# Moving the first stage boundary of a hand-scheduled loop in front of one projection, with two loads and a store behind it

## The chip, the cores and the metric

The kernel runs on one core of one Trainium2 chip. The metric is the device time of one execution in microseconds (us); the number used is the median of several runs. The core has five instruction streams that run beside each other: TensorE (PE, with its weight loads shown as PEld), VectorE (DVE), ScalarE (ACT), GpSimd (POOL) and SyncE (SP). They meet only through semaphores. SP computes nothing here: it issues loads from DRAM and waits for them. ACT and POOL also issue some transfers.

## The reference

An input `x` of 2048 tokens with 640 features goes through two mixers, and a gate per token blends them: `out = g * a + (1 - g) * b`. Mixer `b` is a sliding, dilated attention. Mixer `a`, which takes most of the time, works through 64 segments of 32 tokens, one after the other, with 8 memory rows that each segment hands to the next:

```python
for s in range(n_seg):
    h = concat([mem, x[:, 32*s : 32*s+32, :]])             # 8 + 32 rows of 640
    q, k, v = h @ Wq, h @ Wk, h @ Wv                       # 32 heads of 192 each
    p = softmax(where(mask, q @ k.T * scale, -1e9))
    o = (p @ v) @ Wo
    mem = o[:, :8, :]
    outs.append(o[:, 8:, :])
```

Since `mem` comes out of the whole segment, segment s + 1 can't begin its projections before segment s has ended.

## The kernel before, in words

Mixer `b` runs first and leaves its share of the result in DRAM (`bsc_dram`). A pre-pass then computes, for all segments at once, the projections of the last 8 tokens of each segment (the "z" rows, `zpk_dram`). What is left per segment is a block of 32 rows, which the method `part_a` works through with the function `segment(prev, s, nxt, looped)`: segment 0 straight, then a loop over 62 segments, then the last one straight, then the output projection of the z rows (`part_z`). Only the loop has stages.

Within a segment the 6144 columns of Q, of K and of V come in three thirds of 2048. `m_qk(i, kcs)` is a projection on PE: i = 0, 2, 4 are the thirds of Q and i = 1, 3, 5 the thirds of K. For each of the five 128-row chunks (kc) of the weights it issues a group of four matmuls that run side by side on the array (line 708). `c_qk(i)` is ACT's copy of the result out of PSUM (line 715), `t_qk(i)` the DVE transpose of it into the layout that attention reads (lines 725 and 728). `m_v(t, kcs)` (line 805) and `c_v(t)` (line 813) do the same for V. Attention is done in two halves h of the heads: `scores(h)` (line 759), `e_exp(h)` (lines 767 and 768), `e_sum(h)` (row sums on PE, line 783), `e_norm(h)` (lines 791 to 796), `pv_half(h)` (lines 829 and 835), and `o_group` is the output projection (line 868).

Not all weights fit on the core. 21 pieces, of 192 or 256 KB, are streamed from DRAM in every segment through a ring of seven buffers `wst`. `release(keys)` marks a buffer free after the last matmul that reads it, and at that place in the program `pump()` puts SP's load of the piece that comes seven places later in the list `STREAM` (line 463). So a load belongs to the place in the program where an older piece is used up, and SP issues it once PE has got there. The second K third, `m_qk(3)`, uses up the pieces ("k", 1, 0, 0) and ("k", 1, 3, 1); the two loads that it sets off bring ("v", 1, 1, 0) and ("v", 1, 4, 1), which `m_v(1)` reads in its second and its last chunk.

The order on every engine is the order of the program text (`manual_schedule`); nothing is rearranged. Semaphores are set back in turns: the loop body has four stages, split by three calls of `stage` (each is a `stage_boundary`) and by the loop's own edge. An engine may enter a stage only when all five engines have reported that they are through with everything of the stage two before it, landed transfers included. The line where an engine makes that report is given by `done(engine, ...)` (a `previous_stage_wait`): there it waits for its own work of the stage before the present one and reports. `done(SP)` thus waits for the landing of the loads that SP issued in that stage. In the trace the instructions of the boundaries and of `done` have the line of the loop, 993. Stage 0 runs from the loop's edge to the first boundary (line 912), stage 1 to the second (line 929), stage 2 to the third (line 960), stage 3 to the edge.

Around the change: `load_vz(s)` loads the z rows of V for `pv_half` (issued by POOL, line 644), `store(prev)` stores the mixed output rows of the segment before (issued by ACT, line 672) from the tile `aG`, which `mix` fills on DVE early in the segment.

Of the kernel before, what the change touches and what calls it, by code (L numbers as in the profile page):

```python
# [26 lines left out]
class _K:  # L27
# [558 lines left out]
    def part_a(self):  # L586
        nc, tc, KC, S = self.nc, self.tc, self.KC, self.S
# [3 lines left out]
        with ctx:  # L591
# [51 lines left out]
            def load_vz(s):  # L643
                nc.gpsimd.dma_start(vz[:], row(self.zpk_dram, s)[:, 768:1152])
# [21 lines left out]
            def store(s, last=False):  # L666
                dst = self.out2d[bass.ds(32 * s, 32), :].rearrange("t (j f) -> j t f", j=4)
                if last:
                    for jj in range(4):
                        nc.scalar.dma_start(dst[jj, 0:24], a4[32 * jj:32 * jj + 24, 0:160])  # L670
                else:
                    nc.scalar.dma_start(dst, a4[:, 0:160])
# [5 lines left out]
            def segment(prev, s, nxt, looped=False):  # L678
# [3 lines left out]
                def stage(*engines):  # L682
                    if looped:
                        tc.stage_boundary()
                    done(*engines)

                def done(*engines):
                    if looped:
                        for e in engines:
                            tc.previous_stage_wait(e)  # L690


                def burst(ms):
                    if looped and len(ms) > 1:
                        key = ms[-1].ins.name
                        for m in ms[:-1]:
                            tc.no_tile_sem_insts.add(m.ins.name)
                            tc.add_to_no_dep_group(key, m.ins)
                        tc.declare_fence(ms[-1].ins, group=key)

                def m_qk(i, kcs):
                    p, m = i // 2, "qk"[i % 2]
                    if i not in pqs:
                        pqs[i] = Ms[i % 2] if p == 1 or i == 4 else X[:, i % 2]
                    pq = pqs[i]
                    for kc in kcs:
                        sl = self.qk_columns((m, p, kc))
                        burst([nc.tensor.matmul(pq[32 * j:32 * j + 32, :], lhsT=hT[:, kc, :], rhs=sl[j],  # L708
                                                start=(kc == 0), stop=(kc == KC - 1), tile_position=(0, 32 * j),
                                                skip_group_check=True) for j in range(4)])  # L710
                        self.release(self.parts((m, p, kc)))

                def c_qk(i, part=None):
                    if part is None:
                        nc.scalar.copy(st[i], pqs[i])  # L715
                    elif part == 0:
                        nc.scalar.copy(st5[0], pqs[i][:, 0:256].rearrange("p (b x) -> p b x", b=4))
                    else:
                        nc.scalar.copy(st5[1], pqs[i][:, 256:512])

                def t_qk(i, part=None):

                    p = i // 2
                    if i % 2 == 0:
                        nc.vector.transpose(P[p][:, 1:5, :, :].rearrange("p b c i -> p c b i"), st[i])  # L725
                    else:
                        c0, c1 = (16 * p % 32, 16 * p % 32 + 16) if part is None else (8 * part, 8 * part + 8)
                        nc.vector.transpose(KT[:, c0:c1, :].rearrange("p c k -> p (c k)"),  # L728
                                            st[i] if part is None else st5[part])
# [178 lines left out]
                t_qk(0); t_qk(1)  # L908
                m_qk(2, range(KC)); c_qk(2); t_qk(2)
                done(SP)  # L910
                m_qk(3, range(KC)); c_qk(3); t_qk(3)
                stage(POOL)
                if prev is not None:
                    load_vz(s)
                    store(prev)
                m_qk(4, range(KC))
                done(PE, ACTE, DVE)
                m_qk(5, (0, 1, 2))
# [70 lines left out]
            ctx.enter_context(tc.manual_schedule(engines=set(ALL)))  # L989
            self.start_stream()  # L990
            segment(None, 0, 1)
            self.sent -= len(STREAM)
            with tc.For_i(0, nseg - 2, 1, hint_engines=(), iteration_sync="staggered", head_align_engines=ALL, name="seg") as i:
                ahead = self.sent
                segment(i, i + 1, i + 2, True)
                self.sent -= len(STREAM)
                assert self.sent == ahead
            segment(nseg - 2, nseg - 1, None)

            def last():  # L1000
# [116 lines left out]
```

## Time and profile before

| what | value |
|---|---|
| median of 3 runs | 1722.83 us (1720.89 to 1736.27) |
| the profiled execution | 1735.46 us, span of its core 1733.6 us |
| granted TensorE clock, mean | 0.978 |
| matmuls | 37477 |
| moved over the span | 438.32 MB, 253 GB/s on average |

A line of the profile names the engine, the source line, the operation and the tiles (written <- read). In a list of waits, "A L1 <- B L2: 86.2, 58, 1.5" says that A, before its instruction of L1, waited for B's L2 86.2 us in all, 58 times, 1.5 us at the longest; "issue" as releaser means that the profile shows no instruction on which it waited: the engine's own sequencer had not handed the instruction over. A "q" after an engine is its sequencer. In a timeline the columns are start and duration in us, engine, line, operation, tiles and count, and in brackets the idle time before. The busy time of matmuls is modelled: four side by side, of 0.38 us each, start every 0.22 us.

### The profile page before, as it was taken

How to read it: one execution, taken by the hardware profiler on the slowest of the kernel's cores; microseconds unless marked ns; L12 is line 12 of the kernel's file. 1: busy time of each engine (PE TensorE's matmuls, PEld its weight loads, DVE VectorE, ACT ScalarE, POOL GpSimd, SP SyncE). 2: the span in 40 equal slices, each digit the busy share in tenths (PEclk: the TensorE clock that was granted, in tenths of full speed). 3: DMA queues.
4: the chain of work that ended last, by engine and by line, in shares of the span. 5: the costliest groups of instructions: out<-in, count | busy, mean ns of one | idle time of the engine just before them, and what ended most of it. 6: DMA issues, size and time to landing. Idle time of an engine off the chain costs nothing. (4 is left out here: it accounts for less than half of the span.)

```text
span 1733.6 us, 91514 instructions
## 1 busy us (share of the span) xinstructions
PE 1488.5 (86%) x37477; PEld 846.2 (49%) x37477; DVE 745.1 (43%) x1808; ACT 721.8 (42%) x1737; POOL 143.7 (8%) x275
## 2 busy tenths in 40 slices
PE   6898997985789889888888898888888888888879
PEld 3454553432345455545545555555554455454447
DVE  4556532222344444444444444444444444444420
ACT  3766631211244444444444444444444444444340
POOL 4001000000100000001000000000100000010000
PEclk9999998998899999999999999999999999999989
DMA  6931079598689989899998998999999899988881
GB/s 165 217 89 48 30 184 283 135 259 250 198 284 313 300 294 310 297 292 290 303 298 289 303 306 298 299 296 307 298 301 299 285 300 297 297 289 293 269 221 27
DMA packets 438730, 438.32 MB, mean 253 GB/s; under 512 B 194172, under 2 KB 306820, under 8 KB 438660
## 3 DMA queue, kind: packets, MB, share of 16 engines
q1 hardware_dynamic: 344344, 395.02, 72.1%
q10 hardware_dynamic: 87148, 29.72, 7.0%
q0 software_dynamic: 7168, 12.60, 2.0%
q8 instruction: 51, 0.84, 0.2%
q14 instruction: 19, 0.16, 0.0%
HBM read 402.83 MB, written 39.48 MB: 255 GB/s over the span
## 5 line engine op out<-in xcount | busy, mean ns | idle before, releaser
L708 PEld LDWEIGHTS <-aH 128*32 128x32 bf16 x7680 | 193.4, 97 | 266.1 <-issue 63.0
L805 PE MATMUL psm<-wlate_v,aH 128*32 128x512 bf16 x3200 | 253.6, 381 | 0.0
L868 PEld LDWEIGHTS <-aP 128*32 128x32 bf16 x6144 | 162.4, 96 | 60.0 <-ACT aP L847 18.8
L708 PE MATMUL psx<-wlate_k,aH 128*32 128x512 bf16 x1920 | 191.4, 386 | 0.0
L868 PE MATMUL psm<-wlate_oa,aP 128*32 128x384 bf16 x2560 | 167.0, 327 | 0.0
L708 PE MATMUL psx<-wres_q,aH 128*32 128x512 bf16 x1152 | 95.7, 393 | 78.3 <-issue 30.1
L715 ACT CAST aP<-psx 128x512 bf16<-128x512 f32 x128 | 68.7, 589 | 224.5 <-PE psx L708 224.5
L728 DVE STREAM_TRANSPOSE aK<-aP 128x512 bf16<-128x512 bf16 (+1 forms) x256 | 142.6, 557 | 15.8
L708 PE MATMUL psx<-wst,aH 128*32 128x512 bf16 x768 | 138.8, 385 | 3.0 <-DMA wst<-wscr 3.0
L868 PE MATMUL psm<-wst,aP 128*32 128x384 bf16 (+1 forms) x896 | 128.1, 305 | 6.4 <-DMA wst<-wscr 6.0
L725 DVE STREAM_TRANSPOSE aP<-aP 128x512 bf16<-128x512 bf16 x128 | 91.1, 711 | 95.8 <-ACT aP L715 95.7
L868 PE MATMUL psm<-wlate_ob,aP 128*32 128x256 bf16 x2688 | 125.7, 273 | 0.7 <-issue 0.7
L805 PE MATMUL psm<-wst,aH 128*32 128x512 bf16 x640 | 125.1, 383 | 0.0
L805 PEld LDWEIGHTS <-aH 128*32 128x32 bf16 x3840 | 91.0, 97 | 63.3 <-issue 1.8
L708 PE MATMUL psm<-wlate_q,aH 128*32 128x512 bf16 x1408 | 105.2, 379 | 1.2 <-ACT aP L715 1.0
L847 DVE CAST aP<-psx 128x128 bf16<-128x128 f32 (+2 forms) x192 | 75.5, 421 | 64.2 <-PE psx L835 64.0
L768 DVE TENSOR_TENSOR aK<-aK,aSel 128x224 bf16<-128x224 bf16 x128 | 35.3, 276 | 151.3 <-ACT aK L767 151.3
L847 ACT CAST aP<-psS 128x384 bf16<-128x384 f32 (+2 forms) x192 | 65.3, 374 | 79.6 <-PE psx L835 77.9
L708 PE MATMUL psm<-wst,aH 128*32 128x512 bf16 x512 | 98.1, 379 | 0.0
L783 PE MATMUL psS<-aK,aSel 128*32 128x160 bf16 (+1 forms) x1024 | 36.1, 216 | 70.5 <-DVE aK L728 59.9
L813 ACT CAST aP<-psm 128x512 bf16<-128x512 f32 x128 | 75.4, 589 | 49.1 <-PE psS L759 49.1
L767 ACT ACTIVATE aK<-psS 128x224 bf16<-128x224 f32 x128 | 46.1, 360 | 117.7 <-PE psS L759 117.7
(164 smaller groups left out, 2762.3 us busy)
## 6 DMA issues: line engine op xcount, KB each, us to landing
wst<-wscr SPq DMA_DIRECT2D x965, 256.0 KB, 4.0
wst<-wscr SPq DMA_DIRECT2D x384, 192.0 KB, 3.2
aP<-zpk_dram SPq DMA_DIRECT2D x64, 192.0 KB, 2.9
zpk_dram<-ZS ACTq DMA_DIRECT2D x5, 2048.0 KB
aVz<-zpk_dram POOLq DMA_DIRECT2D x64, 96.0 KB, 4.5
wlate_k<-in_A_Wk_dram SPq DMA_DIRECT2D x8, 512.0 KB
wres_q<-in_A_Wq_dram SPq DMA_DIRECT2D x7, 512.0 KB
wst<-in_A_Wk_dram SPq DMA_DIRECT2D x14, 256.0 KB
```

The costliest lines, as they stand in the source:

```text
L708: burst([nc.tensor.matmul(pq[32 * j:32 * j + 32, :], lhsT=hT[:, kc, :], rhs=sl[j], start=(kc == 0), stop=(kc == KC - 1), tile_position=(0, ...
L715: nc.scalar.copy(st[i], pqs[i])
L725: nc.vector.transpose(P[p][:, 1:5, :, :].rearrange("p b c i -> p c b i"), st[i])
L728: nc.vector.transpose(KT[:, c0:c1, :].rearrange("p c k -> p (c k)"), st[i] if part is None else st5[part])
L767: nc.scalar.activation(E, pSs[h][:, :, 0:112], ACT.Exp, scale=scale_a)
L768: nc.vector.tensor_tensor(out=E, in0=E, in1=self.mask[h].unsqueeze(1).to_broadcast([128, 2, 112]), op=ALU.mult)
L783: ms.append(nc.tensor.matmul(out, lhsT=self.bones[:, j:j + 1].to_broadcast([128, 32]), rhs=rhs, start=(z == 0), stop=(z == 1), tile_positi ...
L805: burst([nc.tensor.matmul(pvs[t][32 * j:32 * j + 32, :], lhsT=hT[:, kc, :], rhs=sl[j], start=(kc == 0), stop=(kc == KC - 1), tile_position ...
L813: (nc.vector.tensor_copy if t == 0 else nc.scalar.copy)(Px[t], pvs[t][:])
L847: (nc.scalar.copy, nc.vector.tensor_copy)[g](x.rearrange("p (j c q) -> p j c q", j=2, q=32), pairs[g][:, :, 0:240].rearrange("p j (c q) -> ...
L868: ms.append(nc.tensor.matmul(pso[part][32 * jj:32 * jj + 32, 0:n], lhsT=oT_slot(R // 2, j, 3 * (R % 2) + t), rhs=self.o_weights(osl, part, ...
```

## The change

In `segment`, the first boundary, `load_vz` and `store` stand in front of the second K third instead of behind it:

```diff
                 m_qk(2, range(KC)); c_qk(2); t_qk(2)
                 done(SP)
-                m_qk(3, range(KC)); c_qk(3); t_qk(3)
                 stage(POOL)
                 if prev is not None:
                     load_vz(s)
                     store(prev)
+                m_qk(3, range(KC)); c_qk(3); t_qk(3)
                 m_qk(4, range(KC))
                 done(PE, ACTE, DVE)
```

So `m_qk(3)`, its copy, its transpose and the two loads that its `release` calls issue go from stage 0 to stage 1. On ACT's queue the store is issued ahead of `c_qk(3)` and not behind it; on POOL's queue nothing else lies between the two places; on SP's queue the boundary now comes ahead of the two loads. The calls `done(PE, ACTE, DVE)`, `done(SP)` and `done(POOL)` keep their places. The straight segments, which have no stages, change only in the order of the store and `c_qk(3)` on ACT.

## The prediction

> **What bounds the kernel now.** I read first the page's engine shares, then stretches of the loop, then the waits inside it, and last one repetition as a timeline, with what SP and PE do on the loop's line.
>
> ```profile
> PE 1488.5 (86%) x37477; PEld 846.2 (49%) x37477; DVE 745.1 (43%) x1808; ACT 721.8 (42%) x1737; POOL 143.7 (8%) x275
> ```
>
> PE leads, and is idle for 14% of the span. The next view sums each engine's busy time over a stretch: 1100 us of the loop, and one repetition (559.2 to 578.1) which I use as the specimen.
>
> ```profile
> 500.00:1600.00 1100.00, 966.66 (x29588) 556.50 (x29581) 506.05 (x1338) 482.10 (x1281) 95.65 (x176) 1.00 0.91 298
> 559.20:578.10 18.90, 16.59 (x508) 9.55 (x508) 8.71 (x23) 8.29 (x22) 1.62 (x3) 1.00 0.94 304
> ```
>
> The clock is full (1.00), the DMA engines are busy 0.91 of the time, PE is idle about 2 us of 18.9. The view of the instructions on the tile aVz gives the repetition:
>
> ```profile
> L644 POOL DMA_DIRECT2D aVz<-zpk_dram x58: 541/543/557, 510.3 to 1585.2; - x58
> ```
>
> 57 periods in 1074.9 us: 18.86 us each, 62 in all. Where PE's idle time lies, by the list of waits over the same 1100 us, and then SP's own list:
>
> ```profile
> POOL aVz L644 <- issue: 378.9, 58, 7.9
> ...
> PEld L783 <- issue: 86.2, 58, 2.2
> ...
> PE psS L783 <- DVE aK L728: 57.5, 57, 1.6
> ```
> ```profile
> SPq L993 <- DMA wst<-wscr: 160.6, 178, 2.2
> ```
>
> The costliest stop of PE's weight loads (the second row), 86.2 / 58 = 1.49 us per repetition, is ahead of `e_sum(0)` (line 783), the first PE work behind the second boundary, and its releaser is the sequencer. SP in turn loses 160.6 us in its `done` calls, on landings. The specimen shows how the two hang together. SP's and PE's instructions of line 993 around the second boundary, and the timeline:
>
> ```profile
> L993 SPq EVENT_SEMAPHORE  x3: 28/28/28, 568.5 to 568.6; - x3
> L993 PEldq EVENT_SEMAPHORE  x2: 51/51/51, 568.7 to 568.9; - x2
> ```
> ```profile
> 567.41 0.60 PE L805 MATMUL psm<-wlate_v,aH 128*32 128x512 bf16 x8
> 567.90 0.96 DVE L728 STREAM_TRANSPOSE aK<-aP 128x256 bf16<-128x256 bf16 x2
> ...
> 568.93 0.15 PEld L783 LDWEIGHTS <-aSel 128*32 128x32 bf16 x8 [1.41 <-issue]
> 568.96 0.28 PE L783 MATMUL psS<-aK,aSel 128*32 128x160 bf16 x8 [0.94 <-DVE aK L728]
> 568.97 0.69 DVE L813 CAST aP<-psm 128x512 bf16<-128x512 f32 x1
> ...
> 569.05 0.40 PE L805 MATMUL psm<-wst,aH 128*32 128x512 bf16 x2
> ...
> 569.72 0.38 PE L805 MATMUL psm<-wst,aH 128*32 128x512 bf16 x2
> ...
> 570.17 0.21 DVE L796 TENSOR_TENSOR aK<-aK,psS 128x64 bf16<-128x64 bf16 x1
> ...
> 571.29 0.10 PEld L829 LDWEIGHTS <-aP 32*128 32x128 bf16 x4 [0.19 <-ACT aP L813]
> ```
>
> SP reports at 568.6, PE passes at 568.7 to 568.9, `e_sum` starts at 568.96. The two matmul groups from 567.41 were through by 567.41 + 2 x 0.22 = 567.85: PE lost 1.11 us. On which landing did SP wait? The loads of `m_qk(3)`, then the four earlier ones of stage 0 (view of the tile wst, with the time from issue to landing):
>
> ```profile
> L463 SPq DMA_DIRECT2D wst<-wscr x2: 319/320/320, 563.2 to 563.9; - x2
> ...
> DMA to landing us min/median/max: 4.2/4.4/4.6
> ```
> ```profile
> L463 SPq DMA_DIRECT2D wst<-wscr x4: 319/320/365, 560.3 to 562.4; - x4
> ...
> DMA to landing us min/median/max: 3.5/3.8/4.0
> ```
>
> 563.9 + 4.6 = 568.5, the start of SP's three instructions to the tenth. The four others had landed by 562.4 + 4.0 = 566.4. So the second boundary opens when the later load of `m_qk(3)` lands, and that load is one of the two that the change takes out of stage 0.
>
> **The change part by part.** *Second boundary.* SP's `done` has then only the four loads to wait for. It reaches them after its last load of `m_qk(5)`:
>
> ```profile
> 566.81 0.32 SPq L463 DMA_DIRECT2D wst<-wscr  x1
> ```
>
> 566.81 + 0.32 = 567.13, plus some 0.15 for its instructions: 567.3, past 566.4, so nothing is left to wait for. From SP's last instruction to the matmul it takes 0.33 us (568.63 to 568.96): `e_sum` could start at 567.6, and PE gets there at 567.85. The whole stop goes; SP and PE are both moved by the stop below, so the margin of 0.25 stays. Scaled from the specimen (stop 1.41) to the mean (1.49), PE gains 1.11 + 0.08 = 1.19 us per repetition.
>
> *First boundary.* It was free, and is so no longer. The timeline and, below it, line 993 on SP and PE:
>
> ```profile
> 562.75 0.38 PE L708 MATMUL psm<-wst,aH 128*32 128x512 bf16 x2
> ...
> 563.11 0.59 ACT L715 CAST aK<-psm 128x512 bf16<-128x512 f32 x1
> ...
> 564.00 0.54 POOL L644 DMA_DIRECT2D aVz<-zpk_dram  x1 [6.53 <-issue]
> 564.05 0.59 ACT L715 CAST aP<-psm 128x512 bf16<-128x512 f32 x1 [0.36 <-PE psm L708]
> ...
> 564.35 0.57 ACTq L672 DMA_DIRECT2D out_dram<-aG  x1
> ...
> 564.94 0.71 DVE L728 STREAM_TRANSPOSE aK<-aP 128x512 bf16<-128x512 bf16 x1
> ...
> 565.56 0.35 PE L759 MATMUL psS<-aP,aK 128*32 128x40 bf16 x14
> ```
> ```profile
> L993 SPq EVENT_SEMAPHORE  x3: 17/28/278, 562.7 to 562.8; - x3
> ```
> ```profile
> L993 PEldq EVENT_SEMAPHORE  x2: 51/51/51, 563.1 to 563.3; - x2
> ```
>
> SP reports at 562.8 + 0.28 = 563.08 and PE's sequencer passes at 563.1 to 563.3, while the array has `m_qk(3)` (from 562.75) to do, handed over before. Behind the boundary, `m_qk(3)` starts 0.33 after SP's report, at 563.41: PE stands still for 0.66 us. Queued behind it are all later matmuls; ACT (`c_qk(3)`), DVE (`t_qk(3)`) and SP's two loads wait for them. Lower bound: without SP's 0.28, 0.38. Upper bound 0.9: POOL, too, is let go by this boundary, and its longest wait, 7.9, is 1.4 above the mean; one repetition in six like that adds 0.24. I take 0.66, since POOL's mean, 378.9 / 58 = 6.53, is the specimen's.
>
> *Store and load.* POOL's load stays where it is, at the opening of the boundary. ACT's store comes earlier: it takes 0.57 us from about 563.11 + 0.30, so to 563.98, and `c_qk(3)` is wanted only at 564.05 + 0.66. Cost nothing; without that cover it would be 0.57. `t_qk(3)` then ends near 566.1, where `scores(0)` starts at 565.56 + 0.66 = 566.2.
>
> *What is late next.* DVE's chain moves 0.66 later while PE comes 0.53 earlier. `c_v(0)` would end at 568.97 + 0.69 + 0.66 = 570.3 and the second multiplication of `e_norm(0)`, 0.7 after the copy in the present (570.17 + 0.21 - 569.66), at most at 571.0. `pv_half(0)` wants it by 571.29 - 0.53 = 570.76, the start of the part that waits for ACT's copy anyway. Since today's 0.7 holds a wait for ACT, the cost lies between 0 and 0.25; I take 0.05.
>
> Sum per repetition: -1.19 + 0.66 + 0.05 = -0.48 us; times 62, -30 us. From the profiled 1735.46 that is 1705.5; the median of the runs lies 12.6 lower, so 1693.
>
> At one place the Trainium skill speaks against this. "DMA: Bandwidth & Descriptors", section on the anatomy of one DMA, fits a transfer by 2.0 us plus bytes over 436 GB/s, measured on the GpSimd path; for 256 KB that is 2.6 us, an estimate from that page. By it the two loads would land at 566.5, and the sum would be the loss alone, the third rival below. The measured 4.2 to 4.6 us, under load, is against it and decides.
>
> **The rivals.** *The V pieces come too late.* The two loads are issued 0.66 later, at 563.9 and 564.54, and by the same 4.2 and 4.6 land at 568.1 and 569.1. `m_v(1)` wants them at 569.05 - 0.53 = 568.5 and 569.72 - 0.53 = 569.2, so the second has 0.1 to spare. The four loads behind them are slower still:
>
> ```profile
> L463 SPq DMA_DIRECT2D wst<-wscr x4: 320/346/373, 564.9 to 566.8; - x4
> ...
> DMA to landing us min/median/max: 4.4/4.8/4.9
> ```
>
> With 0.4 us more the gain falls to about 0.1 x 62 = 6 us: 1717. For it: a DMA share of 0.94 in the specimen. Against: the four loads ahead of them are issued when they are now, so these two find a shorter queue. Chance 0.17. The specifications in the Trainium skill's "DMA: Bandwidth & Descriptors" give a core about 358 GB/s from HBM; an estimate from that leaves the specimen's 304 GB/s a sixth of room.
>
> *Slower: the second boundary is not the last releaser.* The profile itself puts part of the stop on the transposes of `t_qk(5)` (57.5 us, the third row of the waits). If `e_sum` needs them, it starts at 567.90 + 0.96 + 0.66 = 569.52, 0.56 later than now, and the change costs 35 us: 1758. It decides as soon as the transposes end behind the boundary. Against it, another repetition, where SP reported early:
>
> ```profile
> 643.96 0.96 DVE L728 STREAM_TRANSPOSE aK<-aP 128x256 bf16<-128x256 bf16 x2
> ...
> 644.51 0.28 PE L783 MATMUL psS<-aK,aSel 128*32 128x160 bf16 x8 [0.43 <-DVE aK L728]
> ```
>
> `e_sum` started 0.4 us before the transposes ended. That leaves this case 0.10.
>
> *Slower still: SP's report at 568.6 does not hang on the two loads.* Then only the first stop and the 0.05 are left, 0.71 x 62 = 44 us: 1767. The landing that agrees with SP's wake-up to the tenth speaks against it: 0.02.
>
> *The first stop does not come about*, because PE's queue still holds enough work: then the gain is 1.14 x 62 = 71 us, 1652. But only `m_qk(2)` stands ahead of the boundary, and it is over at 562.75. Chance 0.03.
>
> **How the numbers follow.** My forecast has 0.68. Its bounds are a first stop of 0.38 to 0.9 and 0 to 0.25 at `pv_half(0)`: -0.81 to -0.04 us per repetition, so 1673 to 1720, mostly under 1705. With the late V pieces at 1717 the range 1672 to 1724 leaves out the other cases (0.15) and a little more, under 2 in 10. A measurement tells about 1% (17 us) from no change. Faster by more: 0.66, nearly all of the forecast and the last rival. Within 1%: 0.21, the late V pieces and the weak end of the forecast. Slower: 0.13, the two slower rivals and a trace of the forecast.
>
> **What would show it.** Right: PE's wait on issue at line 783 falls from 86.2 us to nearly nothing, and a new one of about 0.66 us per repetition stands at line 708 ahead of `m_qk(3)`; SP's total on landings falls by some 70 us; the period is near 18.4 us. The V rival shows as waits of line 805 on wst, the slower one as line 783 waiting for line 728 with no boundary in between. I'd be wrong if the first stop is well above 0.9 us, or if the stop at the second boundary only moves to the third or to the loop's edge.

## The result, and the profile after

| | median us | runs |
|---|---|---|
| kernel before, the three runs above and one more | 1726.15 (1720.89 to 1736.27) | 4 |
| changed kernel | 1703.41 (1699.32 to 1704.8) | 4 |

The ratio is 0.985, with a 95% interval of 0.982 to 0.988: faster, by less than 2%. In a later comparison of the same two kernels it was 0.984 (0.980 to 0.987). The profiled execution took 1704.8 us (span 1703.3); for it the prediction had 1705.5. For the median it had 1693, which is 10 us too low. The medians lie 22.7 us apart (27.4 in the later comparison), the profiled executions 30.7, because the kernel before was profiled in one of its longer executions: 1735.46 us, where its four runs go from 1720.89 to 1736.27.

The page and the stretches of the changed kernel, then the row of the tile aVz that marks the repetitions:

```profile
PE 1488.0 (87%) x37477; PEld 853.1 (50%) x37477; DVE 739.5 (43%) x1808; ACT 715.8 (42%) x1737; POOL 143.3 (8%) x275
```
```profile
500.00:1570.00 1070.00, 963.43 (x29484) 560.83 (x29483) 500.93 (x1337) 475.42 (x1278) 94.23 (x174) 1.00 0.94 305
```
```profile
L644 POOL DMA_DIRECT2D aVz<-zpk_dram x58: 541/541/557, 511.0 to 1562.0; - x58
```

PE has the same work (1488.0 against 1488.5 us) in less time. The 57 periods between the 58 loads take 1051.0 us, so 18.44 us each where it was 18.86. The share of the DMA engines rises from 0.91 to 0.94, since the same bytes move in a shorter loop.

The list of waits of the changed kernel (engine and line <- releaser: us in total, times, longest), over 1070 us of the loop, and SP's own list:

```profile
PEld L708 <- issue: 76.6, 75, 2.4
...
DVE aK L728 <- ACT aP L715: 35.3, 58, 1.7
...
PE psm L708 <- issue: 22.7, 58, 1.2
...
PEld L805 <- issue: 13.4, 55, 0.6
...
PE psm L805 <- DVE aP L813: 8.4, 37, 0.2
...
PE psm L805 <- DMA wst<-wscr: 2.4, 8, 0.5
```
```profile
SPq L993 <- DMA wst<-wscr: 76.4, 127, 2.1
```

The reader is to see what is gone and what is new. No wait at line 783 is left in the list; it had cost PE's weight loads 86.2 us and the array 57.5. SP waits 76.4 us for landings in its reports, where it waited 160.6. New is the array's wait on issue at line 708, once per repetition (58 times): the stop at the first boundary. New and small are waits at line 805: on the sequencer, on a landing, and on DVE's copy of line 813.

One repetition of the changed kernel, from 819.40 to 837.76, shows both boundaries. First SP's and PE's instructions of line 993 around the first and around the second, then the timeline:

```profile
L993 SPq EVENT_SEMAPHORE  x11: 17/17/28, 822.9 to 823.5; - x11
L993 PEldq EVENT_SEMAPHORE  x2: 51/51/51, 823.1 to 823.2; - x2
...
L993 SPq EVENT_SEMAPHORE  x2: 28/28/28, 827.7 to 827.8; - x2
L993 PEldq EVENT_SEMAPHORE  x2: 51/51/51, 827.8 to 828.0; - x2
```
```profile
823.35 0.39 PE L708 MATMUL psm<-wst,aH 128*32 128x512 bf16 x2 [0.24 <-issue]
...
823.67 0.57 ACTq L672 DMA_DIRECT2D out_dram<-aG  x1
823.94 0.55 POOL L644 DMA_DIRECT2D aVz<-zpk_dram  x1 [6.91 <-issue]
...
827.96 0.60 PE L805 MATMUL psm<-wlate_v,aH 128*32 128x512 bf16 x8
...
828.34 0.96 DVE L728 STREAM_TRANSPOSE aK<-aP 128x256 bf16<-128x256 bf16 x2
828.39 0.27 PE L783 MATMUL psS<-aK,aSel 128*32 128x160 bf16 x8
...
828.48 0.38 PE L805 MATMUL psm<-wst,aH 128*32 128x512 bf16 x2
...
829.41 0.69 DVE L813 CAST aP<-psm 128x512 bf16<-128x512 f32 x1
...
830.15 0.39 PE L805 MATMUL psm<-wlate_v,aH 128*32 128x512 bf16 x2 [0.25 <-DVE aP L813]
```

At the second boundary SP reports at 827.8 and PE's sequencer passes by 828.0; the groups from 827.96 keep the array busy, and `e_sum(0)` starts at 828.39 behind them with no idle time in brackets. It starts while the transposes of line 728, which end at 828.34 + 0.96 = 829.30, have hardly begun. At the first boundary the array stands still ahead of `m_qk(3)`. And at 830.15 the third V projection waits for `c_v(0)`, which ends at 829.41 + 0.69 = 830.10: both use one PSUM tile.

The trace has the start of each of the 508 matmuls of a repetition. Counted from the first, these are the mean starts of some of them over the first 61 repetitions of the loop (the last row is the mean distance of two repetitions):

| matmul | before, us | changed, us | gained since the row above |
|---|---|---|---|
| 73rd: first of `m_qk(3)` | 3.46 | 4.02 | -0.56 |
| 205th: first of `e_sum(0)` | 9.79 | 9.07 | +1.28 |
| 213th: second chunk of `m_v(1)` | 9.89 | 9.27 | -0.10 |
| 277th: first of `m_v(2)` | 11.25 | 10.86 | -0.23 |
| 285th: first of `pv_half(0)` | 11.81 | 11.43 | -0.01 |
| 297th: second group of `pv_half(0)` | 12.14 | 11.57 | +0.19 |
| 508th: last | 17.80 | 17.24 | -0.01 |
| next repetition | 18.96 | 18.48 | -0.08 |

The sum is 0.48 us per repetition, and 0.48 x 62 = 30 us: the two profiled executions, which the table compares, differ by 1735.46 - 1704.8 = 30.7.

### The profile page after: what moved, and what is told of

Same layout as the page of the kernel before. It is cut to its first block, busy times and chain, and to the rows that moved or that the text cites. A ratio compares the mean times of both kernels' runs of the same rounds, so it can differ in the third digit from the quotient of the medians.

```text
span 1703.3 us, 91642 instructions
## 1 busy us (share of the span) xinstructions
PE 1488.0 (87%) x37477; PEld 853.1 (50%) x37477; DVE 739.5 (43%) x1808; ACT 715.8 (42%) x1737; POOL 143.3 (8%) x275
## 5 line engine op out<-in xcount | busy, mean ns | idle before, releaser
L708 PEld LDWEIGHTS <-aH 128*32 128x32 bf16 x7680 | 193.7, 97 | 304.5 <-issue 114.6
L805 PEld LDWEIGHTS <-aH 128*32 128x32 bf16 x3840 | 100.1, 96 | 82.9 <-issue 15.3
L715 ACT CAST aP<-psm 128x512 bf16<-128x512 f32 x128 | 74.6, 583 | 62.9 <-PE psm L708 58.9
L813 ACT CAST aP<-psm 128x512 bf16<-128x512 f32 x128 | 75.3, 589 | 55.1 <-PE psS L759 45.5
L644 POOL DMA_DIRECT2D aVz<-zpk_dram x64 | 35.0, 547 | 682.2 <-issue 413.3
```

The costliest lines, as they stand in the source:

```text
L805: burst([nc.tensor.matmul(pvs[t][32 * j:32 * j + 32, :], lhsT=hT[:, kc, :], rhs=sl[j], start=(kc == 0), stop=(kc == KC - 1), tile_position ...
L813: (nc.vector.tensor_copy if t == 0 else nc.scalar.copy)(Px[t], pvs[t][:])
```

## The experiments

There were ten runs on one chip, in three groups; beside them the kernel before had medians of 1732.6, 1730.4 and 1731.4 us. The theory: PE's second stop hangs on the landing of the two loads, and only that is gained; the first stop is the price of putting PE's boundary early. The rivals: it is the boundary's place that gains; or the place of the store and of the Vz load has a part in it. Each diff is against the kernel that its sentence names. In the kernels with `hold`, lines behind 711 have numbers higher by one (784 for 783, 806 for 805), and the loop's line is 995 or 996.

The starts in one table, as above (mean over 61 repetitions, us; for the two versions that ran twice, the second run). Issues and landings of transfers below are medians over the same repetitions, counted from the same first matmul:

| matmul | change | loads alone | later load alone | report earlier | boundary alone | copy ahead | store alone | store in stage 0 |
|---|---|---|---|---|---|---|---|---|
| 73rd `m_qk(3)` | 4.02 | 3.47 | 3.48 | 3.90 | 4.07 | 3.98 | 3.99 | 3.46 |
| 205th `e_sum(0)` | 9.07 | 8.57 | 8.72 | 8.95 | 9.11 | 9.02 | 9.04 | 9.22 |
| 213th `m_v(1)` | 9.27 | 8.97 | 8.82 | 9.29 | 9.25 | 9.21 | 9.19 | 9.32 |
| 277th `m_v(2)` | 10.86 | 10.65 | 10.51 | 10.89 | 10.88 | 11.11 | 10.80 | 11.07 |
| 285th `pv_half(0)` | 11.43 | 11.35 | 11.17 | 11.45 | 11.52 | 11.67 | 11.44 | 11.66 |
| 297th `pv_half(0)` | 11.57 | 11.54 | 11.33 | 11.68 | 11.62 | 12.03 | 11.54 | 11.94 |
| 508th, last | 17.24 | 17.21 | 17.00 | 17.35 | 17.27 | 17.71 | 17.20 | 17.63 |
| next repetition | 18.48 | 18.33 | 18.14 | 18.60 | 18.40 | 18.96 | 18.38 | 18.84 |

**The loads alone.** The kernel before, with PE's boundary left where it was; only the two loads of `m_qk(3)` go behind it.

```diff
-                m_qk(3, range(KC)); c_qk(3); t_qk(3)
+                m_qk(3, range(KC), hold=(0, 3)); c_qk(3); t_qk(3)
                 stage(POOL)
+                self.release(self.parts(("k", 1, 0))); self.release(self.parts(("k", 1, 3)))
```

> Boundary, load and store stand where they stood before; only the two loads that the second K third sets off are issued behind the boundary, so that they belong to stage 1. Theory (the second boundary waited for these two landings): the stop ahead of line 783 (1.19 us per repetition) goes, and no stop comes at the first boundary. About 0.4 us comes back, as the first of the two V pieces lands at some 9.0 us of the repetition and would now be wanted at 8.75: 0.8 x 62 = 50 us faster than before, about 1676 us (1666 to 1690). Rival (the gain came from the place of the boundary or from the earlier store, not from the stage of the loads): no change, 1726 us.

Measured: 1687.13 us, ratio 0.973 (0.971 to 0.975), less than the change takes. Neither stop is there: `m_qk(3)` starts at 3.47 as before the change, and `e_sum(0)` at 8.57, 1.22 us earlier than before. That would be worth 1.22 x 62 = 76 us, and 45 were gained. The list of waits of this kernel says where the rest went:

```profile
PEld L806 <- issue: 39.0, 91, 1.5
...
PE psm L806 <- DMA wst<-wscr: 15.6, 36, 1.0
```

PE now comes early enough to run into its V pieces. The first of them is issued at 4.30 and lands at 8.82, and the 213th matmul, which reads it, could start right behind `e_sum(0)`, near 8.66. It starts at 8.97. The second piece, which the 227th matmul is the first to read, costs another 0.2 us: that matmul starts 0.21 us after the 226th, where it was 0.01 in the kernel before. So the landing of the loads is the gain, as the theory says, and the rival of the late V pieces is real once the first stop is gone.

**The later load alone.** The same with only the second of the two loads behind the boundary. It ran twice, the second time beside the changed kernel.

```diff
-                m_qk(3, range(KC)); c_qk(3); t_qk(3)
+                m_qk(3, range(KC), hold=(3,)); c_qk(3); t_qk(3)
                 stage(POOL)
+                self.release(self.parts(("k", 1, 3)))
```

> As the first run, but only the later of the two loads is issued behind the boundary; the earlier one stays in stage 0. Theory: the second boundary then waits for the earlier load, which lands at about 8.4 us of the repetition instead of 9.4. The stop ahead of line 783 falls from 1.19 to about 0.2 us, and the first V piece has landed by then: 0.8 to 0.9 us per repetition, 50 to 55 us faster than before, 1671 to 1680 us. Rival (something else holds the second boundary): 1726 us, or what the first run gives.

> The boundary left where the kernel before has it, only the later of the two loads behind it, as in the third experiment. If PE's boundary is the part of the change that costs and the load the part that gains, this is 10 to 20 us below the changed kernel of the same chip, ratio to the kernel before 0.968 to 0.978. If the third experiment's lead came from its runs, it is within 5 us of the changed kernel.

Measured: 1684.81 us, ratio 0.972 (0.967 to 0.977), and the second time 1680.89, ratio 0.971 (0.967 to 0.975), against 1702.99, ratio 0.984 (0.980 to 0.987), of the changed kernel that ran beside it. The waits of the second run:

```profile
PEld L708 <- issue: 27.7, 26, 1.8
...
PEld L806 <- issue: 23.4, 68, 1.1
...
PEld L784 <- issue: 17.6, 34, 1.4
...
PE psm L806 <- DMA wst<-wscr: 2.6, 9, 0.6
```

The weight loads' wait at line 708 is 27.7 us and not 76.6: no stop ahead of `m_qk(3)`. A little of the second stop is left (17.6 us, 34 times), since in 34 repetitions SP's report there still waits for the landing of the first load, and the V pieces come nearly in time, because the first load now keeps its early place: issued at 3.91, landed at 7.99. The second piece still costs some 0.15 us. The gain on the kernel before is 47.8 and 49.5 us, a little under the 50 to 55 that the first expectation had. This is the fastest version found, though its lead over the loads alone (0.973) lies inside the intervals, and PE's boundary has not moved in it. The lead over the change, 22.1 us, is what the table gives: (18.48 - 18.14) x 62 = 21 us.

**The boundary alone.** The changed kernel with the Vz load and the store put back behind the projection. It ran twice, the second time beside the changed kernel, which ran once more for this.

```diff
                 stage(POOL)
+                m_qk(3, range(KC)); c_qk(3); t_qk(3)
                 if prev is not None:
                     load_vz(s)
                     store(prev)
-                m_qk(3, range(KC)); c_qk(3); t_qk(3)
```

> The change with the load of the z rows and the store left behind the second K third: the boundary alone is moved. Theory: as the whole change, 1703 us; the store, now again behind the two loads, leaves the first V piece up to 0.15 us earlier, at most 9 us faster (1694 to 1705). Rival (the earlier store is what helped): back towards 1726 us.

> The changed kernel once more, on the same chip as the three below, so that they can be set beside it and not only beside the kernel before. Expected ratio to the kernel before 0.982 to 0.988, as before.

> The boundary alone in front of the projection, the load of Vz and the store behind it, as in the second experiment. If having the store and the Vz load ahead of the two V loads costs what the V pieces' latency showed (about 0.1 us at each of two pieces, on the path in some repetitions), this is 3 to 8 us below the changed kernel of the same chip. If the 5 us of the first comparison were scatter between chips or runs, the two agree within 2 us.

Measured: 1698.38 us, ratio 0.981 (0.979 to 0.984), and 1697.03, ratio 0.981 (0.977 to 0.984), against the change's 1702.99 (ratio given above). Both times it is 5 to 6 us under the change; the intervals overlap, so on their own they do not settle it. The POOL load is issued at the same time in both kernels (4.43 and 4.45 in the second pair). What differs is the store, which ACT issues at 4.16 in the change and at 5.40 here, and the landing of the V pieces: 8.93 and 9.63 with the store ahead, 8.75 and 9.47 with it behind.

**The store alone.** The changed kernel with the store put back behind the projection, the Vz load in front.

```diff
                     load_vz(s)
-                    store(prev)
                 m_qk(3, range(KC)); c_qk(3); t_qk(3)
+                if prev is not None:
+                    store(prev)
```

> The changed kernel with the store alone put back behind the projection; the Vz load stays in front. If the 5 to 6 us by which the boundary alone beat the whole change come from the store, which ACT issues 1.2 us earlier in the changed kernel, this is as fast as the boundary alone, ratio 0.979 to 0.983, and the first V piece lands 0.1 to 0.3 us earlier than in the changed kernel. If they come from the Vz load, the ratio is that of the changed kernel, 0.983 to 0.987.

Measured: 1695.44 us, ratio 0.978 (0.975 to 0.981). The first V piece lands at 8.77. With the store behind it is as fast as the boundary alone, so it is the store that costs the change some 6 us, and not the Vz load. The changed kernel did not run beside this one; by the ratios of all these runs (0.978 to 0.981 with the store behind, 0.984 and 0.985 for the change) the store costs 5 to 11 us. How much of it is the V piece is less clear: the last matmul comes only 0.04 us earlier than in the change, and the rest, (18.48 - 17.24) - (18.38 - 17.20) = 0.06 us, is gained between it and the next repetition.

**The store in the stage before.** The kernel of the later load alone, with the store in front of the second K projection, where in that kernel the boundary has not yet come.

```diff
+                if prev is not None:
+                    store(prev)
                 m_qk(3, range(KC), hold=(3,)); c_qk(3); t_qk(3)
                 stage(POOL)
                 self.release(self.parts(("k", 1, 3)))
                 if prev is not None:
                     load_vz(s)
-                    store(prev)
```

> The kernel of the third experiment (boundary where it was, the later load behind it) with the store in front of the second K projection, so in stage 0. If an early store is what costs, this is 4 to 7 us slower than the third experiment was, ratio 0.974 to 0.977. If not, the ratio stays at 0.971 to 0.972.

Measured: 1725.09 us, ratio 0.996 (0.994 to 0.998). A loss of 4 to 7 us was expected, and some 44 came (1725.09 against 1680.89). SP's list of waits in this kernel names the reason, and the weight loads' wait at the second boundary is back:

```profile
SPq L996 <- DMA wst<-wscr: 80.9, 124, 1.7
...
SPq L996 <- DMA out_dram<-aG: 44.1, 47, 2.9
```
```profile
PEld L784 <- issue: 52.3, 57, 3.0
```

The store now belongs to stage 0, and SP's reports wait for its landing (44.1 us, 47 times in the list, which covers 1070 us; 50 of 61 repetitions at the second boundary). ACT issues it at 4.01, it lands at 8.51, and `e_sum(0)` starts at 9.22 and not at 8.72. The same store, at about the same time, costs the changed kernel no such stop, because there the boundary went in front of it. This experiment was meant for the queues and showed the stages: the expectation had not counted the store among what the boundary waits for.

**SP's report earlier.** The changed kernel with `done(SP)` in front of the second Q projection, to see whether the first stop can be shortened.

```diff
-                m_qk(2, range(KC)); c_qk(2); t_qk(2)
                 done(SP)
+                m_qk(2, range(KC)); c_qk(2); t_qk(2)
                 stage(POOL)
```

> The change with SP's report for stage 3 put ahead of the second Q third, so that SP no longer issues that third's load before it reports. If the first stop (0.55 us per repetition in the changed kernel) is set by SP's own queue, it falls by 0.2 to 0.3 us: 12 to 18 us faster than the change, about 1688 us. If it is set by the landing of the load issued at the loop's edge, it stays: within 5 us of 1703, and the load pushed behind the report lands later for nothing.

Measured: 1712.89 us, ratio 0.988 (0.987 to 0.990), which neither theory had: some 10 us slower than the change, with intervals that just touch. The waits of this kernel:

```profile
PEld L805 <- issue: 26.0, 64, 1.7
...
PE psm L708 <- issue: 14.9, 32, 1.8
...
PE psm L805 <- DMA wst<-wscr: 9.2, 16, 1.5
```

The wait ahead of `m_qk(3)` falls from 22.7 us, 58 times, to 14.9, 32 times, but the mean start of `m_qk(3)` moves by 0.12 us alone. The report now stands ahead of the loads that `m_qk(2)` sets off; where it waits for a landing, they wait behind it on SP's queue, and so does all that SP issues after them. The first V piece is issued at 4.63 and not at 4.34, and PE's weight loads of line 805 wait for 26.0 us and not 13.4. The 0.12 us are lost again by the 213th matmul (9.29 against 9.27).

**The copy ahead.** The changed kernel with DVE's `c_v(0)` in front of the second part of `t_qk(5)`.

```diff
-                c_qk(5, 1); t_qk(5, 1)
+                c_qk(5, 1)
                 done(SP)
                 m_v(0)
                 c_v(0)
+                t_qk(5, 1)
```

> The changed kernel with DVE's copy c_v(0) ahead of the second part of t_qk(5), so 0.45 us earlier. If the third V projection waits, behind scores(1), for this copy (both use the same PSUM tile), the stop of line 805 behind line 759, 16 us in sum over the loop, goes. In its place scores(1) waits for the transpose, which now ends 0.3 to 0.6 us later, by about 0.3 us per repetition: a new stop ahead of line 759 of some 20 us, and the time within 10 us of the changed kernel. If the third V projection waits for something else, the stop of line 805 stays and the kernel is about 20 us slower than the changed one.

Measured: 1734.23 us, ratio 1.002 (0.9995 to 1.004): 31 us above the change, where at most 10 were expected. The waits of this kernel hold no row of line 805 on the copy any more, but these two:

```profile
PEld L759 <- DVE aK L728: 25.7, 50, 0.6
...
PE psS L759 <- DVE aK L728: 20.2, 49, 0.5
```

So the releaser was named rightly: with the copy ahead, the third V projection no longer waits for it. Its first matmul starts 0.11 us after the last one of `scores(1)`, as in the kernel before; in the changed kernel it was 0.33 us. The price was not named rightly: the transpose now holds up `scores(1)`, everything behind follows (`pv_half(0)` at 11.67 and not 11.43), and its second group starts 12.03 - 11.67 = 0.36 us after the first and not 0.14.

## Why the prediction came out

*The second boundary* was read rightly. The stop was put down to the landing of the later load of `m_qk(3)`. In the kernel before, that landing ends SP's wait at this boundary in all 61 repetitions, so the specimen spoke for the loop. With the loads gone from that stage the wait is gone, whether PE's boundary moves (the change) or not (the loads alone). The gain up to `e_sum(0)` was put at 1.19 us and measured as 1.28.

*The first boundary* was mis-sized a little: 0.66 forecast, 0.56 measured. In every repetition `m_qk(3)` starts 0.29 us after the end of SP's report (the prediction took 0.33 from the second boundary). What varies is the report. The specimen had in it a wait of 0.28 us for a landing; in the changed kernel 26 of the 61 repetitions have such a wait, of over 0.1 us, and `m_qk(3)` starts at 4.20 in their mean. In the other 35 it starts at 3.90. The row of waits agrees: 22.7 / 58 = 0.39 us, counted from the modelled end of the last group, and since groups of 0.38 start every 0.22 us, 0.16 more of lost time, 0.55 in all.

*`pv_half(0)`* was forecast to cost 0.05, since DVE's chain comes later and PE earlier. It gained 0.19: its second group starts 0.14 us behind its first, where it was 0.33. By the order of the rows this belongs with the loss ahead of it: `m_v(2)` has brought PE to `pv_half(0)` 0.23 later, by which time its inputs are nearer.

*The third V projection* was missed. The prediction followed `c_v(0)` to `e_norm(0)` and `pv_half(0)`, but not to `m_v(2)`, which needs the PSUM tile that the copy empties. With PE earlier and DVE later they meet, for 0.23 us per repetition; moving the copy took the wait away and showed whose it was.

*The rival of the late V pieces* is in part true: the 213th matmul loses 0.10 us against `e_sum(0)`, where the rival had 0.4 for the two pieces. The argument against it, that the two loads would find a shorter queue, fell. From issue to landing the later piece took as long as before (4.64 us in both medians), and the first longer, 4.50 against 4.18. In the second trace of the changed kernel the later one took 4.55 and the first 4.39. The store had gone ahead of them. "Issuing engines are not separate DMA queues", a section of the page "DMA: Bandwidth & Descriptors" of the Trainium skill, says that transfers from ACT, SP and GpSimd run on the same 16 DMA engines and interleave. The traces agree: with the store behind, in three runs, the later piece needs 4.35 us; in the two runs of the changed kernel it needs 4.55 and 4.64. The shorter queue thus shows for the later piece once the store is out of its way, and the change itself hid it. The prediction had costed the move of the store at nothing and looked for its price on ACT's queue alone.

*The transposes* as last releaser, the slower rival, fell: `e_sum(0)` starts 0.9 us before they end. So did the other one: SP's report hung on the two loads. And the first stop did come about, in every repetition.

Between the two profiled executions the sum was right to 0.01 us per repetition, and that is luck: its misses cancel: too little gained at the second boundary (0.09), too much lost at the first (0.10) and at `pv_half(0)` (0.24), against 0.34 at the two V projections and 0.08 at the loop's edge, for which it had nothing. Either side alone is worth 0.42 x 62 = 26 us. Which executions were profiled is luck too. The medians, 22.7 and 27.4 us apart, make 0.37 and 0.44 us per repetition, and the step from the profile to the median, 12.6 us down, did not hold for the changed kernel: its profiled execution lies 1.4 above its median.

One stop of the same kind was overlooked: the loop's edge. In 53 of the 61 repetitions of the changed kernel, and in 57 before, the next repetition's first matmul starts 0.46 us after the landing of the last load that SP issues ahead of the third boundary, so that landing opens the edge. From the start of the last matmul to the next repetition it takes 1.24 us in the mean and 0.65 at the least. An estimate from these two is that moving that load behind the third boundary could bring up to 0.6 us per repetition; this was not tried.

What stays open: why the way from the last matmul to the next repetition is 1.21 to 1.25 us in the four kernels with the early store and 1.12 to 1.18 in the others, the one before among them. The load that opens the edge takes 3.8 to 4.0 us in all of them. It is issued 3.14 to 3.19 us ahead of the last matmul in the four and 3.20 to 3.22 in the others, which is a part of the difference.

## What to carry to other kernels

Where a boundary waits for landings, ask first which transfer lands last, and move that transfer to the other side by itself; moving the boundary takes along the compute, which then pays for a stop of its own. Here moving one load brought 48 to 49 us, and moving PE's boundary with the projection, two loads and the store 23 to 27. A transfer that changes its place in the program has two prices that its issue time does not show: the stage whose boundary waits for its landing, and the transfers of other engines that it goes ahead of.

## What the runs showed of the hardware

The changed kernel's list of DMA issues (count, size, median us from issue to landing) has for the large loads into `wst`:

```profile
wst<-wscr SPq DMA_DIRECT2D x965, 256.0 KB, 4.0
```

The store of 40 KB takes longer, 4.8 us from issue to its last landing (median over the same 61 repetitions). Its landing shows as 5 events in the trace, the first 1.0 us after the issue, where a load into `wst` has 16, the first 1.9 to 3.9 us after it. The Trainium skill's "DMA: Bandwidth & Descriptors", section on why a DMA increments its semaphore by 16, has a rule that fits: a transfer issued by ACT or SP runs on as many DMA engines, up to 16, as divide the outermost dimension of both its sides, and the issuing sequencer adds what is missing to 16 at once. The store's outermost dimension is 4, so one early event and 4 landings. That it takes long because it runs on few engines was not tried.
